# One edit to a hand-placed schedule: recurrent groups a slot sooner, and a new order around the first MLP products

## The chip, the cores and the metric

The kernel runs on one core of a Trainium2 chip. The metric is the device time of one execution in microseconds (us), less being better. Five instruction engines take part: TensorE (PE in the profile; its weight loads are PEld), VectorE (DVE), ScalarE (ACT), GpSimd (POOL) and SyncE (SP), which here issues the DMA transfers.

## The reference

Two parts follow one another. The first is an mLSTM cell over `(batch, heads, tokens, width) = (4, 8, 768, 40)`; per token, with stabilised gates:

```python
m_new  = np.maximum(f_gate + m, i_gate)
f_stab = np.exp(f_gate + m - m_new); i_stab = np.exp(i_gate - m_new); m = m_new
C = f_stab * C + i_stab * (v outer k)
n = f_stab * n + i_stab * k
y = sigmoid(o_gate) * (C @ q) / np.maximum(np.abs(n @ q), 1.0)
```

The second takes the result as `x` of shape `(4, 768, 320)`:

```python
mixed = np.real(fft(fft(x, axis=1), axis=2))
u  = x + mixed
un = (u - mean) / np.sqrt(var + 1e-06)
out = u + np.maximum(un @ w_ch1, 0.0) @ w_ch2      # 320 -> 1280 -> 320
```

All is float32.

## The kernel before

**The stages.** Each of the four batches (b = 0 to 3) runs through a recurrence, a Fourier mix and an MLP. The recurrence is done in six chunks (c = 0 to 5) of 128 tokens. For b = 1 to 3 it works on halves of 64 tokens: `halves_scores` and `halves_to_state` (products into the bank `ps`), `halves_from_state`, `halves_between` and `halves_from_chunk` (into the bank `ph`). All these products are issued by the helper `product`, at L582, so that the trace has them under that line. One chunk's products, together with the `from` products of an earlier chunk, make a group of small products of 40 or 64 rows and 40 or 64 columns.

What surrounds a group runs on other engines. ACT does `mlstm_exp` (L551, the weights W, eight instructions for the eight heads) and the gate in `mlstm_tanh` (L748, L650). POOL does `mlstm_scale_q` (L563, qg), `mlstm_scale_v` (L569, vw), `mlstm_mask` (L578) and the decay of the state (L705, C). DVE does `halves_add` (L712, C), `halves_weigh` (L717, W) and `mlstm_finish` (L768 to L772 and L759, which turn `ph` into `x`). SP issues the loads (qk, kvt, W, so, Gb).

**The mix** has sequence transforms (`mix_seq`, `mix_tail`, L944 and L956, banks pz and pzt; those of pzt have 64 columns), feature transforms (`mix_feat`, L990, bank pu), `mix_add` (DVE, L1003 to L1014: adds pu to x and takes the statistics), `mix_center` (ACT, L1028, uc), `mix_turn` (PE, L1039, transposes into ph or put) and `mix_turn_out` (ACT, L1044, uT).

**The MLP** of batch 0 is `mlp_in` (L1137, with `mlp_in_rests` for the last 64 features, L1120 through `rest_products`), `mlp_relu` (ACT, L1155) and `mlp_out` (L1275). Batches 1 to 3 use five blocks i = 0 to 4 with fewer products on sums of operands. `mlp_block` (L1203) has steps 0, 1, 2, 2.5 and 3: its products write four banks `pm`, ACT copies them out (L1218, L1232, L1241 and, with the relu, L1254), DVE adds (L1209), step 2.5 issues sixteen 64-feature products (L1120), and `mlp_relu_in_place` (L1258) follows. The output is `mlp_out_pair` (L1332) with three parts n of four steps, on `hidden_sums` (L1317, S1 to S4) and with `residual` (DVE, L1281).

**Weights.** They come in pieces that are stored packed: `load` (SP, L453), `take` (DVE, L463 and L465), `convert` (ACT, L471) and `join` (DVE, L478, L481 and L485). The list `when` gives the slots of take, convert and join of each piece.

**The order** is written by hand. `at(slot, phase, fn)` notes a step, and `run` issues all steps in sorted order; every engine's queue is then in that order:

```python
    def run(end=None):
        for key in sorted(plan):
            if end is None or key[0] < end:
                for fn, args in plan.pop(key):
                    fn(*args)

    EVAC, FILL, MAIN, FILL_PE = range(4)
```

Batch 0's `mlp_in` has slots 31 to 50 and its `mlp_out` 51 to 62. The blocks of batch 1 have 63 to 82 (i=0 is 63 to 66, i=1 67 to 70), its `mlp_out_pair` 83 to 94, the blocks of batch 2 95 to 114. `plan_halves` starts at slot 32 for b=1, 54 for b=2 and 86 for b=3, with three slots for a chunk. So b=1's recurrence runs beside the first batch's MLP input, b=2's beside its output and the first blocks of batch 1 (about 105 to 193 us), b=3's beside the output of batch 1 and the blocks of batch 2 (about 193 to 277 us).

Of the kernel before, what the change touches and what calls it, by code (L numbers as in the profile page):

```python
# [20 lines left out]
NT = S // L  # L21
NP = H // 2
# [35 lines left out]
def kernel(  # L58
# [68 lines left out]
    def at(slot, phase, fn, *args):  # L127
        plan.setdefault((slot, phase), []).append((fn, args))
# [7 lines left out]
    EVAC, FILL, MAIN, FILL_PE = range(4)  # L136
# [682 lines left out]
    def plan_halves(b, s0, stride=3):  # L819
        at(s0 - 2, FILL + 0.7, halves_start, b)  # L820
        for c in range(NT):
            s = s0 + stride * c
            end = c == NT - 1
            t = 22 + 2 * c if b == 1 and c < 3 else s - 6
            at(t, FILL, mlstm_load, b, c)
            at(t, FILL, mlstm_load_max, b, c)
            at(*((t, FILL + 0.02) if (b, c) == (1, 0) else (t + 1 if c < 2 or b > 1 else s - 5, FILL)), mlstm_load_decay, b, c)
            at(s - 2, FILL, mlstm_load_o, b, c)
            at(s - 2, FILL + 0.1, mlstm_scale_q, b, c)
            at(s - 2, FILL + 0.15, halves_alone, b, c)  # L830
            at(s - 1, FILL, mlstm_scale_v, b, c)
            early = (b, c) == (1, 0)
            at(*((27, FILL + 0.227) if early else (s - 1, FILL)), mlstm_exp, b, c, 0)
            at(*((32, EVAC + 0.15) if early else (s - 1, FILL + 0.5)), mlstm_exp, b, c, NP)
            at(s, FILL, mlstm_mask, b, c)
            at(s, FILL_PE + 2.05, halves_scores, b, c)
            at(s, FILL_PE + 2.5, halves_to_state, b, c)
            for i in range(2):
                at(s + i, FILL + 0.05, halves_decay, b, c, i)
                at(s + 1 + i, FILL - 0.2, halves_add, b, c, i)  # L840
            at(s + 1, FILL, halves_weigh, b, c)
            if end:
                for fn, phase in (((halves_from_state, -0.3), (halves_between, -0.2), (halves_from_chunk, -0.05)) if b == 1 else
                                  ((halves_from_state, 0.1), (halves_between, 0.15), (halves_from_chunk, 0.3))):
                    at(s + (3 if b == 1 else 4), MAIN + phase, fn, b, c)
            else:
                at(s + 3, FILL_PE, halves_from_state, b, c)
                at(s + 3, FILL_PE + 0.5, halves_between, b, c)
                at(s + 3, FILL_PE + 3, halves_from_chunk, b, c)
            at(s + 3, FILL_PE + 0.6, mlstm_tanh, b, c)  # L850
            at(s + 4, FILL + 0.05 if b == 1 else MAIN + 0.4, mlstm_finish, b, c)

# [213 lines left out]
    def plan_mix(b, s0, x_done, s_feat, s_add, s_turn):  # L1068
        for j in range(TG):
            p = TG - 1 - j  # L1070
            if b == 0:
                at((17, 18, 18.5)[j], FILL + (0.1, 0.07, 0.3)[j], mix_fold, b, p)
                s, phase = ((17, 3), (19, 3), (22, 4))[j]
                for i, part in enumerate(((1,), (0,)) if j == 1 else ((0, 1),)):
                    at(s, FILL_PE + phase + 0.1 * i, mix_seq, b, p, part)
                at(*((18, FILL_PE + 0.2) if j == 0 else (s, FILL_PE + phase + 0.2)), mix_tail, b, p)
            else:
                at(x_done[j] + (b > 1 and j == TG - 1), FILL + 0.5 if b < 2 else FILL_PE + 0.2, mix_fold, b, p)
            if b > 0 and j == 0:
                for step in range(2):  # L1080
                    at(*((x_done[-1], FILL + 0.55) if b == 1 else (x_done[-1] + 2 + 2 * step, FILL_PE + 0.25)),
                       mix_fold_again, b, step)
                at(s0, FILL_PE + 4, mix_seq, b, p, (0,))
                at(s0 + 1, FILL_PE + 4, mix_seq, b, p, (1,))
                at(s0 + 2, FILL_PE + 4, mix_tail, b, p)
        for i in range(2):
            at(s0 + 1 if b == 0 else s0 + 1 + i, FILL, mix_seq_out, b, i)
        at(s0 + (1 if b == 0 else 3), FILL + 0.1, mix_tail_out, b)
        for p in range(TG):
            for i in range(3) if b == 0 and p == TG - 1 else ():  # L1090
                at(s_feat[p] + i, FILL_PE + 5.1, mix_feat, b, p, slice(i, i + 1))
            if b == 0 and p == TG - 2:
                at(s_feat[p], FILL_PE + 4.06, mix_feat, b, p, slice(0, 3))
                at(s_feat[p] + 1, FILL_PE + 4.95, mix_feat, b, p, slice(3, 5))
            elif b == 0 and p == 0:
                at(s_feat[p], FILL_PE + 4, mix_feat, b, p, slice(0, 2))
                at(s_feat[p], FILL_PE + 4.04, mix_feat, b, p, slice(2, 3))
            elif b > 0 or p < TG - 1:
                at(s_feat[p], FILL_PE + 4, mix_feat, b, p)
        for c, a, t in zip(ORDER, s_add, s_turn):  # L1100
            at(a, FILL if b < 2 else MAIN + 0.5, mix_add, b, c)
            if b > 0 and c == TG - 2:
                at(a, FILL + 0.15 if b < 2 else MAIN + 0.55, mix_own, b)
            at(*(((32, EVAC + 0.1) if c == 3 else (a, FILL + 0.225) if c in (4, 2) else (t, FILL + 0.1)) if b == 0 else
                 (t, FILL + 0.1)), mix_center, b, c)
            at(t, FILL_PE + (5 if b == 0 or c in ORDER[:4] else -0.1), mix_turn, b, c)
            if b > 0:
                at(t, FILL_PE + 6, mix_turn_out, b, c)
            elif t < s_mlp:
                at(t + 1, FILL + 0.2, mix_turn_out, b, c)  # L1110
            else:
                at(t + 1, EVAC, mix_turn_out, b, c)
# [254 lines left out]
    def plan_mlp(b, s):  # L1367
# [10 lines left out]
        for gr, n in IN_ORDER if b == 0 else ():  # L1378
            for f in (2 * n, 2 * n + 1):
                at(s, MAIN, mlp_in, b, gr, f)  # L1380
                s += 1
            i = IN_ORDER.index((gr, n))
            if i < 4 or i % 2 == 0 or i == 9:
                at(*((s, MAIN + 0.5) if i == 1 else (s - 1, MAIN + (-0.1 if i in (2, 8, 9) else 0.2))), mlp_in_rests, b, i,
                   False)
                if 3 < i < 8:
                    at(s - 1, MAIN + 0.25, mlp_in_rests, b, i + 1, True)
            for f in (2 * n, 2 * n + 1):
                at(s + (i == 1), EVAC, mlp_relu, b, gr, f)
        if b > 0:  # L1390
            for j in range(1, 5):
                at(s - (5, 4, 3, 3)[j - 1], FILL_PE + 0.3, hidden_sums, 0, (j,), 0, NFF // 2 - 2)
# [9 lines left out]
        for gr in groups if b == 0 else ():  # L1402
            for i in range(TG):
# [3 lines left out]
                n = gr * TG + i  # L1407
# [45 lines left out]
        at(66 if n == 3 else 57, FILL + 0.41, out_weight_sums, n)  # L1453

    when = [((2, 0.7), (4, 0.5), None), ((18.5, 0.7), (20, 0.7), (21, 0.6)), ((21.5, 0.7), (23, 0.15), None)]
    when += [((27, 0.16), None, (29, 0.5)), ((30, 0.7), (34, 0.7), (35, 0.6))]
    when += [((s, 0.7), (s + 1, 0.7), (s + 2, 0.6)) for s in (36, 39, 42, 48, 51)]
    pieces = w1_pieces + w2_pieces
    for n, (w, p) in enumerate(zip(when, pieces)):
        if n > 2:  # L1460
            at(when[n - 2][2][0] + 1 if n != 4 else 27, FILL + 0.7, p.load)
        for t, fn in zip(w, (p.take, p.convert, p.join)):
            if t:
                at(t[0], FILL + t[1], fn)
    for part, s in enumerate((7, 10, 13)):
        at(s, FILL - 0.28, pieces[0].join, part)
    for part, (s, phase) in enumerate(((27, 0.13), (27, 0.14), (27, 0.15))):
        at(s, FILL + phase, pieces[2].join, part)
    at(27, FILL + 0.23, pieces[3].convert)

    early = [(3, mlstm_load, 3), (3, mlstm_load_o, 2), (4, mlstm_load, 4), (5, mlstm_load_decay, 3),
             (5, mlstm_load_decay, 4), (7, mlstm_load_o, 3), (7, mlstm_load, 5),
             (11, mlstm_load_decay, 5), (11, mlstm_load_o, 4), (12, load_tables, None), (15, None, 2),
             (11.5, mlstm_load_o, 5)]
# [157 lines left out]
```

## Time and profile before

| | |
|---|---|
| time, median of 3 runs | 383.31 us (382.96 to 384.71) |
| time of the profiled execution | 381.6 us |
| its span | 379.7 us |
| PE busy | 372.2 us, 98% of the span |
| DVE, ACT, POOL busy | 74%, 45%, 35% |
| granted TensorE clock | 1.0 throughout |
| data moved | 43.99 MB, mean 116 GB/s |

The span goes from the first to the last instruction of one profiled execution; its time also holds what lies around the span. "Busy" adds up the instructions of an engine; for PE the ends of the matrix products are modelled. A row of the timeline has the start, the duration, engine, line, operation, output and inputs, tile and shape, and in brackets the idle time ahead of it and who ended it. A float32 product shows as two instructions.

### The profile page before, as it was taken

How to read it: one execution, taken by the hardware profiler on the slowest of the kernel's cores; microseconds unless marked ns; L12 is line 12 of the kernel's file. 1: busy time of each engine (PE TensorE's matmuls, PEld its weight loads, DVE VectorE, ACT ScalarE, POOL GpSimd, SP SyncE). 2: the span in 40 equal slices, each digit the busy share in tenths (PEclk: the TensorE clock that was granted, in tenths of full speed). 3: DMA queues.
4: the chain of work that ended last, by engine and by line, in shares of the span. 5: the costliest groups of instructions: out<-in, count | busy, mean ns of one | idle time of the engine just before them, and what ended most of it. 6: DMA issues, size and time to landing. Idle time of an engine off the chain costs nothing.

```text
span 379.7 us, 11405 instructions
## 1 busy us (share of the span) xinstructions
PE 372.2 (98%) x4602; PEld 274.3 (72%) x4602; DVE 279.4 (74%) x662; ACT 170.9 (45%) x501; POOL 131.7 (35%) x238
## 2 busy tenths in 40 slices
PE   8999998999999999999999999999999999999996
PEld 5888565566677777566588999566588996546996
DVE  8798899899997596787965787878745885245552
ACT  5978766657332224654542054564520233544000
POOL 5665423965695014561602424651300000020000
PEclk9999999999999999999999999999999999999999
DMA  7979499698971244464003534440000001000011
GB/s 203 292 219 344 125 251 269 174 270 246 260 212 38 90 128 128 129 187 139 0 3 93 157 117 130 131 80 3 0 2 35 19 18 36 0 0 2 35 36 35
DMA packets 21760, 43.99 MB, mean 116 GB/s; under 512 B 3508, under 2 KB 9996, under 8 KB 21580
## 3 DMA queue, kind: packets, MB, share of 16 engines
q1 hardware_dynamic: 21708, 43.27, 39.3%
q8 instruction: 36, 0.59, 0.7%
q14 instruction: 16, 0.13, 0.1%
HBM read 39.16 MB, written 4.10 MB: 114 GB/s over the span
## 4 chain that ended last, share of the span: by engine, by line
PE 83%; DVE 5%; POOL 3%; ACT 1%; DMA 1%; issue 1%; POOLq 0%; DVEq 0%
PE po L1332 22%; PE pm L1203 19%; PE po L1275 9%; PE pm L1120 7%; PE ph L582 5%; PE pm L1137 4%; PE ps L582 4%; PE pu L990 3%; PE pz L944 2%; PE put L1039 2%; DMA raw<-in_w 1%; PE hb L582 1%; PE pzt L944 1%; POOL W L578 1%; PE pz L956 1%
## 5 line engine op out<-in xcount | busy, mean ns | idle before, releaser
L1281 DVE SCALAR_TENSOR_TENSOR x<-po,rstd,x 128x160 f32<-128x160 f32 (+1 forms) x69 | 27.1, 394 | 37.6 <-PE po L1332 34.0
L1209 DVE TENSOR_TENSOR h<-h,pm 128x384 f32<-128x384 f32 x60 | 30.5, 549 | 24.1 <-PE pm L1120 10.8
L578 POOL TENSOR_SCALAR_AFFINE_SELECT W<-W 64x512 f32<-64x512 f32 x36 | 28.5, 792 | 42.1 <-ACT W L551 23.2
L1203 PE MATMUL pm<-uT,w_sb 128*128 128x384 f32 x90 | 37.5, 506 | 0.1
L551 ACT ACTIVATE W<-W,colT 128x64 f32<-128x64 f32 x144 | 36.6, 336 | 0.1
L705 POOL TENSOR_TENSOR C<-C,decB 128x164 f32<-128x164 f32 x33 | 18.1, 550 | 49.8 <-DVE C L712 45.6
L1275 PE MATMUL po<-w_sb,h 128*128 128x320 f32 x120 | 33.9, 433 | 0.0
L1120 PE MATMUL pm<-uT,w_sb 64*64 64x384 f32 x320 | 32.7, 497 | 0.0
L563 POOL TENSOR_TENSOR qg<-qk,Gb 128x512 f32<-128x512 f32 x21 | 27.7, 1318 | 8.3 <-DMA Gb<-G_d 7.0
L1063 POOL TENSOR_TENSOR t<-rstd 128x6 f32<-128x6 f32 x12 | 3.7, 311 | 75.5 <-DVE v L1057 75.0
L1137 PE MATMUL pm<-uT,w_sb 128*128 128x384 f32 x80 | 28.9, 499 | 0.6 <-ACT h L1155 0.6
L1275 PEld LDWEIGHTS po<-w_sb,h 128*128 128x128 f32 x120 | 22.4, 190 | 9.1 <-issue 0.3
L1332 PE MATMUL po<-T,S 128*128 128x160 f32 x180 | 27.8, 301 | 0.2 <-DVE x L1281 0.2
L1332 PEld LDWEIGHTS po<-T,S 128*128 128x128 f32 x180 | 25.4, 190 | 1.3 <-DVE x L1281 0.4
L1332 PE MATMUL po<-w_sb,h 128*128 128x160 f32 x180 | 26.3, 300 | 0.0
L1332 PEld LDWEIGHTS po<-w_sb,h 128*128 128x128 f32 x180 | 25.2, 190 | 1.4 <-DVE x L1281 0.3
L1203 PEld LDWEIGHTS pm<-uT,w_sb 128*128 128x128 f32 x90 | 15.5, 189 | 12.8 <-DVE h L1209 5.3
L1258 ACT ACTIVATE h<-h 128x384 f32<-128x384 f32 x45 | 23.1, 520 | 2.9 <-DVE h L1209 2.9
L1120 PEld LDWEIGHTS pm<-uT,w_sb 64*64 64x64 f32 x320 | 10.9, 132 | 16.4 <-issue 13.6
L1137 PEld LDWEIGHTS pm<-uT,w_sb 128*128 128x128 f32 x80 | 14.1, 189 | 11.4 <-issue 1.8
L569 POOL TENSOR_TENSOR vw<-kvt,colT 128x328 f32<-128x328 f32 x23 | 19.3, 839 | 4.0 <-issue 2.2
L582 PE MATMUL ps<-qk 40*64 40x64 f32 (+1 forms) x768 | 19.1, 235 | 0.4 <-DVE C L712 0.4
(254 smaller groups left out, 814.3 us busy)
## 6 DMA issues: line engine op xcount, KB each, us to landing
kvt<-in_kv SPq DMA_DIRECT2D x24, 336.0 KB
qk<-in_qkT SPq DMA_DIRECT2D x48, 160.0 KB
raw<-in_w SPq DMA_DIRECT2D x10, 640.0 KB
Gb<-G_d SPq DMA_DIRECT2D x42, 128.0 KB
W<-M_d SPq DMA_DIRECT2D x36, 128.0 KB
so<-in_o SPq DMA_DIRECT2D x24, 160.0 KB
out<-x SPq DMA_DIRECT2D x23, 160.0 KB
ds_sb<-in_dft_s SPq DMA_DIRECT2D x1, 1158.0 KB
```

What stands on the lines that cost most here:

```text
L551: nc.scalar.activation(out=k.W[:, h, :], in_=M, func=AF.Exp, scale=-1.0, bias=colT[:, c, 0, b * H + h:b * H + h + 1])
L563: nc.gpsimd.tensor_tensor(out=k.qg[:, :, t], in0=k.qk[:, 0, :, t], in1=k.Gb[:, :, t], op=OP.mult)
L578: nc.gpsimd.affine_select(out=W, in_=W, compare_op=OP.is_ge, fill=0.0, base=base, pattern=[[0, H], [-1 if back else 1, LH]], channel_multi ...
L582: nc.tensor.matmul(out, w, x, start=start, stop=True, skip_group_check=True)
L1120: nc.tensor.matmul(banks[i][half(cols)], w1_rest(n)[half(i), half(cols)], u[half(i)], start=start, stop=not start, skip_group_check=True)
L1137: nc.tensor.matmul(k.pm[i], w1_block(ch, f // 2 * 2 + i), u[2 * ch], start=(ch == 0 and not ahead), stop=(ch == 1 and (ahead or n in (2, 8 ...
L1203: nc.tensor.matmul(bank, w, u, start=start, stop=True, skip_group_check=True)
L1209: nc.vector.tensor_tensor(out=h, in0=h, in1=bank, op=OP.add)
L1258: nc.scalar.activation(out=h, in_=h, func=AF.Relu, scale=-1.0)
L1275: nc.tensor.matmul(k.po[m], hidden(gr, f)[:, i * L:(i + 1) * L], w2_sb[:, f, :], start=(f == 0), stop=(f == NFF - 1))
L1281: nc.vector.scalar_tensor_tensor(out=u, in0=po, scalar=k.rstd[:, c:c + 1], in1=u, op0=OP.mult, op1=OP.add)
L1332: nc.tensor.matmul(po, a[:, f], w[:, f], start=start and f == 0, stop=f == half - 1, skip_group_check=True)
```

## The change

Two groups of edits.

*First batch* (recurrence b=1, beside batch 0's `mlp_in`). `mix_center` of c=3 goes from slot 32 to 33. The relus of `mlp_in`'s block i=0 go one slot and phase ahead of where they stood. The exponentials of the second four heads of (b=1, c=0) move from slot 32 to 28, `mlstm_scale_v` of (1, 1) two slots ahead. Of the weights' pieces, piece 2's join goes from 27 to 28, piece 3's take, convert and join from 27, 27 and 29 to 28, 32 and 33, piece 4's take from 30 to 33, piece 5's take from 36 to 35, and the loads of pieces 4 and 5 to 28 and 33. PE's order in this part is the same as before.

*Third and fourth batch* (recurrence b=2 and b=3). All steps of chunks c = 0 to 4 come one slot sooner, with their loads. The `from` products, the tanh and the finish of a chunk follow its new slot, except that c=4's stay where they were (`follow`). The exponentials of c=4 and c=5 come one further slot sooner (`ahead`). PE gets the groups in these places: for b=2, c=0 into `mlp_out`, c=1 beside the products of pzt, c=2 ahead of the mix's first transpose, c=3 right ahead of block i=0, c=4 right behind the 64-feature products (L1120) of block i=0 instead of behind step 3; for b=3, c=0 ahead of pzt, c=1 between step 1 and step 2 of `mlp_out_pair`, c=2 behind step 0 of n=2, c=3 ahead of the block, c=4 behind the 64-feature products.

On ACT the eight exponentials of c=4 then stand ahead of L1218 of block i=0 (they stood between L1232 and L1241), and those of c=5 between L1254 and the first L1258 of block i=1. On DVE of b=3's part, the finish of c=0 and of c=1 come ahead of a `mix_add` that they followed. On SP the stores (L1283) and the loads of a chunk swap places in several cases.

```diff
@@ plan_halves @@
         for c in range(NT):
-            s = s0 + stride * c
+            s = s0 + stride * c - (b > 1 and c < NT - 1)
             end = c == NT - 1
+            follow = s + 3 + (b > 1 and c == NT - 2)
...
-            at(s - 1, FILL, mlstm_scale_v, b, c)
-            early = (b, c) == (1, 0)
-            at(*((27, FILL + 0.227) if early else (s - 1, FILL)), mlstm_exp, b, c, 0)
-            at(*((32, EVAC + 0.15) if early else (s - 1, FILL + 0.5)), mlstm_exp, b, c, NP)
+            at(*((s - 3, FILL + 0.06) if (b, c) == (1, 1) else (s - 1, FILL)), mlstm_scale_v, b, c)
+            early, ahead = (b, c) == (1, 0), int(b > 1 and c >= NT - 2)
+            at(*((27, FILL + 0.227) if early else (s - 1 - ahead, FILL)), mlstm_exp, b, c, 0)
+            at(*((28, FILL + 0.23) if early else (s - 1 - ahead, FILL + 0.5)), mlstm_exp, b, c, NP)
...
-                at(s + 3, FILL_PE, halves_from_state, b, c)
-                at(s + 3, FILL_PE + 0.5, halves_between, b, c)
-                at(s + 3, FILL_PE + 3, halves_from_chunk, b, c)
-            at(s + 3, FILL_PE + 0.6, mlstm_tanh, b, c)
-            at(s + 4, FILL + 0.05 if b == 1 else MAIN + 0.4, mlstm_finish, b, c)
+                at(follow, FILL_PE, halves_from_state, b, c)
+                at(follow, FILL_PE + 0.5, halves_between, b, c)
+                at(follow, FILL_PE + 3, halves_from_chunk, b, c)
+            at(follow, FILL_PE + 0.6, mlstm_tanh, b, c)
+            at(follow + 1, FILL + 0.05 if b == 1 else MAIN + 0.4, mlstm_finish, b, c)
@@ plan_mix @@
-            at(*(((32, EVAC + 0.1) if c == 3 else (a, FILL + 0.225) if c in (4, 2) else (t, FILL + 0.1)) if b == 0 else
+            at(*(((33, EVAC + 0.1) if c == 3 else (a, FILL + 0.225) if c in (4, 2) else (t, FILL + 0.1)) if b == 0 else
@@ plan_mlp @@
-                at(s + (i == 1), EVAC, mlp_relu, b, gr, f)
+                at(*((s - 1, MAIN + 0.3) if i == 0 else (s + (i == 1), EVAC)), mlp_relu, b, gr, f)
@@ weight pieces @@
-    when += [((27, 0.16), None, (29, 0.5)), ((30, 0.7), (34, 0.7), (35, 0.6))]
-    when += [((s, 0.7), (s + 1, 0.7), (s + 2, 0.6)) for s in (36, 39, 42, 48, 51)]
+    when += [((28, 0.2), None, (33, -0.9)), ((33, 0.7), (34, 0.7), (35, 0.6))]
+    when += [((35, 0.65) if s == 36 else (s, 0.7), (s + 1, 0.7), (s + 2, 0.6)) for s in (36, 39, 42, 48, 51)]
...
-            at(when[n - 2][2][0] + 1 if n != 4 else 27, FILL + 0.7, p.load)
+            at({4: 28, 5: 33}[n] if n in (4, 5) else when[n - 2][2][0] + 1, FILL + 0.7, p.load)
...
-    for part, (s, phase) in enumerate(((27, 0.13), (27, 0.14), (27, 0.15))):
+    for part, (s, phase) in enumerate(((28, 0.1), (28, 0.11), (28, 0.12))):
...
-    at(27, FILL + 0.23, pieces[3].convert)
+    at(32, MAIN + 0.35, pieces[3].convert)
```

## The prediction

> **What bounds the kernel now.** I read the page's busy times first, then its chain, then the timeline around the lines that the diff touches. Each line number below is one of the kernel before; from the edit in `plan_halves` on, the changed kernel's are higher by one. b counts batches from 0, c the chunks of a recurrence.
>
> ```profile
> span 379.7 us, 11405 instructions
> PE 372.2 (98%) x4602; PEld 274.3 (72%) x4602; DVE 279.4 (74%) x662; ACT 170.9 (45%) x501; POOL 131.7 (35%) x238
> PE 83%; DVE 5%; POOL 3%; ACT 1%; DMA 1%; issue 1%; POOLq 0%; DVEq 0%
> ```
>
> PE is the bound: 98% of the span, 83% of the chain that ended last. No matrix product is added or removed, so time can only come from PE's waits and from what products cost beside one another. The waits that the timeline states are few, and three lie where the first edits are:
>
> ```profile
> 59.82 0.61 ACT L1028 ACTIVATE uc<-x 128x384 f32<-128x384 f32 x1 [0.78 <-DVE x L1014]
> 60.85 0.55 PE L1039 MATMUL ph<-ident,uc 128*128 128x128 f32 x3 [0.57 <-ACT uT L1044]
> 63.31 0.91 PE L1137 MATMUL pm<-uT,w_sb 128*128 128x384 f32 x2 [0.62 <-ACT h L1155]
> 76.19 0.69 PE L582 MATMUL ps<-qk 40*64 40x64 f32 x32 [0.37 <-DVE C L712]
> ```
>
> The columns are start, duration, engine, line, operation, and in brackets the idle time with its releaser. Other waits are hidden inside a group of products whose first operand was there and whose later one was not. Sixteen 64-feature products (L1120) show it, in block i=0 and in i=1:
>
> ```profile
> 160.10 2.31 PE L1120 MATMUL pm<-uT,w_sb 64*64 64x384 f32 x16
> 169.13 1.55 PE L1120 MATMUL pm<-uT,w_sb 64*64 64x384 f32 x16
> 159.10 2.02 ACT L551 ACTIVATE W<-W,colT 128x64 f32<-128x64 f32 x8
> 161.03 0.46 ACT L1241 COPY h<-pm 128x384 f32<-128x384 f32 x1
> ```
>
> From start to the next start the first is 2.24 and the second 1.34: 0.9 lost, because the copy L1241, which empties the bank that the last of the sixteen write, stood behind eight exponentials (W x8, 2.02). The same group at 244.12 in the next batch loses as much.
>
> **First batch** (recurrence of b=1 beside the first MLP stage). PE's order stays; DVE's and ACT's change. Now DVE does a piece's join and take from 55.27 to 58.50 and only then mix_add of c=2 (58.50 to 59.73); uc of c=2 follows at 59.82. After, that mix_add comes first, 3.2 sooner. By the rows' durations uc ends at 57.6, W x4 (1.05) at 58.65, the turn's copy and both relus (0.86) at 60.3, so the stalls of 0.57 and 0.62 at 60.85 and 63.31 go. from_state of c=0 then starts at 66.6 instead of 67.95 (1.35 sooner). The next from_state, now at 74.69, starts on finish (DVE, ended 74.63); with the piece-4 take behind C and W of c=0, finish ends near 73.8. The third stall (0.37) goes because piece 5's take (L463 and L465, 1.28) no longer precedes that C. The group after it ends at 76.1 instead of 77.60: 1.5 sooner. DVE has no idle from 71.97 to 119.2, so PE cannot keep more than DVE gains; by the same chain piece 5's L478 starts at 74.0 instead of 76.06, a gain of 2.06, which is the upper end. POOL's mask and vw move across the conversions: L478, L481 and L485 take 1.18, 1.31, 1.11 beside POOL and 0.79, 0.81, 0.82 alone, 1.18 in all, of which half may come back (1.2 - 0.6 = 0.6 as the lower end). SP's moved loads (two weight pieces, so) cover ahead of need; a late piece would show as DVE's wait on raw, now 0.64 at 63.78, which is inside that bound. **Taken: -1.4 (from -2.0 to -0.6).**
>
> **Third batch's recurrence (b=2), 150 to 170 us.** Five groups go a slot up. A group's entry costs little: L1275 x10 takes 2.69, and 2.79 ahead of a group; the group's last part (kvt,W) is 0.58 with 128*128 work behind it and 0.46 with 64*64 behind it; pu costs 1.19 after a group and 1.08 else. Group c=1 beside pzt (64 columns) saves 0.3 at most, c=2 0.06, c=4 beside L1120 about 0.2. Each exp comes a slot sooner on ACT: W x8 (2.0) of c=4 is now ahead of L1218 of block i=0, and no longer between L1232 and L1241. That frees the sixteen rests (0.9) and 0.3 ahead of them, but the product behind L1218 waits about 0.65 and the rests' bank waits for an L1209 that now stands behind a finish (1.65), about 0.85. So i=0 gives -0.2 + 1.5 - 1.2 = +0.1. In i=1 the order is now L1218, L1254 (0.49), W x8 (2.0), L1258 (0.5), L1232 (0.46); before, W x8 (165.45 to 167.45) lay beside group c=4, which now is ahead of step 3. The product that needs L1232's bank is wanted 2.6 after step 3 and gets it after 3.5: +0.87. **Sum -0.36 + 0.1 + 0.87 = +0.6 (from -0.4 to +1.5).**
>
> [...]
>
> **Fourth batch's recurrence (b=3), 200 to 250 us.** Group c=0 beside pzt saves 0.25. Group c=1 now stands between steps 1 and 2 of mlp_out_pair, where step 2 lost 0.15 of stated gap and 0.2 inside at 216.63; that goes, -0.35, and 0.07 at joins: -0.67 by 220.75. Then DVE:
>
> ```profile
> 221.62 0.79 DVE L1317 TENSOR_TENSOR S<-h,h 128x640 f32<-128x640 f32 x1
> 224.02 0.37 DVE L1281 SCALAR_TENSOR_TENSOR x<-po,rstd,x 128x160 f32<-128x160 f32 x1
> 223.17 0.71 PE L990 MATMUL pu<-dd_sb,Z 128*128 128x161 f32 x4
> ```
>
> Before, step 2's residual ended at 220.0, mix_add (1.65) ran to 221.6, and pu at 223.17 found its bank free by 1.5. After, step 2 lies behind the group and its residual ends near 221.2; finish of c=0 (1.65, as at 236.38 to 238.02) comes ahead of mix_add, whose last read of the bank ends at 224.1, while pu is wanted at 222.4: 1.7. The next step 0 needs the residual behind S, S (1.57) and C (0.25), 0.1 late: **+1.8** in all. The same pattern, finish of c=1 ahead of mix_add of the last chunk, makes its transpose late: residual at 234.3, then 1.64 + 1.65 + uc 0.6 gives 238.2 against 237.1 wanted, **+1.0**. Block i=0 loses both its stalls (-1.2: its W x8 is early enough) and i=1 gains 0.87. **Sum -0.67 + 1.8 + 1.0 - 1.2 + 0.87 = +1.8 (from 0.2 to 2.6);** the low end has finish in DVE's idle times, where it would cost nothing. From 277 us on no order changes.
>
> **Sum.** -1.4 + 0.6 + 1.8 = +1.0; I take +0.9, since the pu wait gives slack to what is queued behind it. The profiled execution took 381.6 (span 379.7 and 1.9 around it) and so becomes 382.5; the median, 383.31, lies 1.7 above that one, so on its basis 384.2.
>
> **Rivals.** (1) *DVE and ACT run ahead and hide the new waits* (faster): if finish's five small operations fall in DVE's idle slots (0.82 at 219.65, 1.29 at 234.72), b=3 gives -0.67 - 1.2 + 0.87 = -1.0 in place of +1.8 and b=2 its -0.36 + 0.1. With -1.4 that is -2.7: 380.6. Against it: finish stands in order behind a residual that PE makes at 221, not at 219. It decides at pu's start: no gap there, and this is it. (2) *DVE and POOL collide in the first batch* (slower): the gain ahead of 72 us is eaten when vw and the mask meet the moved conversions; two masks cost 2.44 beside them and 1.38 apart, three conversions 3.6 and 2.42, together 2.24, more than the 1.4 taken. With nothing gained there the sum is +2.4: 385.7. It decides if PE reaches the group at 76.19 no sooner than now. For it: DVE has no slack from 71.97 on. (3) *No change*: PE is gapless after 77.6, and the first batch pays what the others cost: 383.3.
>
> [...]
>
> **How the numbers follow.** The forecast has a chance of 0.47, rival 1 0.18, rival 2 0.23, rival 3 0.12. A measurement of this kernel can tell 0.5% (1.9 us) from no change, so the bounds are 381.4 and 385.2. Faster: rival 1 (most of it) and a low tail of the forecast, 0.18. Slower: rival 2 and the upper quarter of the forecast, 0.35. The rest, 0.47, is within. The forecast's own range, with the three sums half way to their ends, is 382.6 to 385.8. The whole range reaches down into rival 1, to 381.3 (its better half, 0.11, is left out), and up past rival 2 (385.7) to 386.4, where the upper ends of the last two sums meet (0.08 is left out above).
>
> **What would show it.** Right: the gaps at 60.85, 63.31 and 76.19 gone and the group after them 1.4 sooner; the sixteen rests of i=0 back at 1.35 in b=3's block; a DVE-released gap of 1.7 before the third pu of b=3's mix; 0.9 inside the products of i=1 of both blocks. Wrong: no gap at that pu, or the same 1.35 us late start of from_state of c=0 as before.

## The result, and the profile after

The changed kernel takes 390.02 us (median of 4 runs, 388.37 to 391.40) against 383.21 us; the ratio is 1.0156, 95% interval 1.0125 to 1.0187. It is slower by 6.8 us; the forecast was 384.2, with 386.4 as its upper end. The profiled execution took 391.4, so it is one of the longer ones; the profile of before (381.6) is one of the shorter ones of its kernel. In the changed kernel all lines from the edit on are higher by one (L1120 is L1121, L1332 is L1333).

The page of after, its span, the busy times and the chain by engine:

```profile
span 389.1 us, 11415 instructions
PE 375.1 (96%) x4602; PEld 277.0 (71%) x4602; DVE 284.9 (73%) x662; ACT 170.7 (44%) x501; POOL 134.9 (35%) x238
PE 80%; DVE 7%; ACT 4%; issue 3%; DMA 3%; POOL 3%; SPq 0%; POOLq 0%; DVEq 0%; ACTq 0%
```

The same 9204 instructions run on PE, but it is no longer gapless: its share of the chain falls from 83% to 80%, and ACT and "issue" rise from 1% each to 4% and 3%. PE's waits in after (engine, line and what it waited for, then sum, count and longest; "issue" is idle time in which PE waited for nothing that the profile shows):

```profile
PE ph L582 <- issue: 1.9, 1, 1.9
PE pu L991 <- DVE x L1012: 1.4, 1, 1.4
PE pm L1204 <- ACT h L1233: 1.4, 2, 0.7
PE ph L582 <- POOL vw L569: 0.9, 1, 0.9
PE put L1040 <- ACT uc L1029: 0.8, 1, 0.8
PE ph L582 <- ACT warm L748: 0.7, 1, 0.7
PE po L1333 <- DVE x L1282: 0.6, 1, 0.6
PE pm L1121 <- DVE h L1210: 0.5, 1, 0.5
```

The two gaps of the first batch are gone, as forecast. These rows answer to the ones at 60.85 and 63.31 before; the third answers to the group at 74.69:

```profile
60.40 0.55 PE L1040 MATMUL ph<-ident,uc 128*128 128x128 f32 x3
60.78 2.10 PE L1138 MATMUL pm<-uT,w_sb 128*128 128x384 f32 x6
74.62 0.60 PE L582 MATMUL ph<-C,qg 40*64 40x41 f32 x26 [0.94 <-POOL vw L569]
```

PE was 1.24 us early at 63 us, but waited 0.94 at 74.62 and started that group only 0.07 sooner than before. Comparing the starts of the same products in both traces gives the whole account (after minus before; a group that was moved counts where both traces have passed it):

| stretch | forecast | trace |
|---|---|---|
| first batch, at 63 us / 77.6 us / 105 us | -1.4 at the end | -1.24 / -0.64 / -0.08 |
| b=2, joins up to block i=0 | -0.36 | -0.2 |
| b=2, block i=0 | +0.1 | +0.65 |
| b=2, block i=1 | +0.87 | +0.73 |
| b=3, c=0 and c=1, up to 221 us | -0.67 | +0.4 |
| b=3, third pu and the po behind it | +1.8 | +2.36 |
| b=3, last transpose | +1.0 | +1.0, and 0.2 at one before |
| b=3, block i=0 | -1.2 | +3.2 |
| b=3, block i=1 | +0.87 | +0.73 |

The rows differ from the forecast by 8.0 us in all. Two thirds of that are two rows: block i=0 of b=3, where 1.2 was to be won and 3.2 was lost, and the stretch to 221 us; the first batch's lost gain is another 1.3. Block i=0 is in this timeline of after, with the table of windows below (window, its length, busy time and count of PE, PEld, DVE, ACT and POOL, then granted clock, DMA share and GB/s):

```profile
252.56 0.51 PE L582 MATMUL ph<-kvt,W 64*64 64x41 f32 x20
254.96 0.65 PE L582 MATMUL ph<-kvt,W 64*64 64x41 f32 x11 [1.89 <-issue]
```

```profile
250.00:252.00 2.00, 2.00 (x65) 1.51 (x67) 1.12 (x3) 0.13 (x1) 1.17 (x3) 1.00 0.93 200
252.00:254.00 2.00, 1.07 (x83) 0.95 (x73) 1.29 (x3) 0.52 (x2) 0.46 (x1) 1.00 1.01 249
254.00:256.00 2.00, 1.04 (x12) 0.96 (x12) 0.24 (x2) 0.00 (x0) 0.00 (x0) 0.71 0.26 62
256.00:258.00 2.00, 2.00 (x4) 1.05 (x4) 1.83 (x4) 0.48 (x1) 1.81 (x2) 0.50 0.04 8
```

PE stops for 1.89 us inside 32 like products for which the profile shows no wait for an operand, while the DMA share is 1.01 (252 to 254 us); then its clock is 0.71 and 0.50 in the two windows up to 258 us. The author's reading, which early_loads below bears out, is that it lacked instructions. The page lists a queue of kind "instruction" (packets, MB, share of the DMA engines):

```profile
q8 instruction: 36, 0.59, 0.7%
```

In the trace each of the 36 packets has 16 KB. That they are PE's is not stated there; taken as PE's alone they give 64 bytes to each of its 9204 instructions and 256 instructions to a packet, an estimate from these numbers. One such packet starts at 243.37 and the next at 252.22; in between PE starts 449 instructions, where no two packets elsewhere in either trace are more than 365 apart. In the kernel before, packets start at 245.87 and at 250.54.

### The profile page after: what moved, and what is told of

Its sections match the earlier page's. It is cut to its first block, busy times and chain, and to the rows that moved or that the text cites. A ratio compares the mean times of both kernels' runs of the same rounds, so it can differ in the third digit from the quotient of the medians.

```text
span 389.1 us, 11415 instructions
## 1 busy us (share of the span) xinstructions
PE 375.1 (96%) x4602; PEld 277.0 (71%) x4602; DVE 284.9 (73%) x662; ACT 170.7 (44%) x501; POOL 134.9 (35%) x238
## 4 chain that ended last, share of the span: by engine, by line
PE 80%; DVE 7%; ACT 4%; issue 3%; DMA 3%; POOL 3%; SPq 0%; POOLq 0%; DVEq 0%; ACTq 0%
PE po L1333 21%; PE pm L1204 17%; PE po L1276 8%; PE pm L1121 7%; PE ph L582 5%; PE pm L1138 4%; PE ps L582 4%; PE pu L991 3%; PE pz L945 2%; DMA so<-in_o 2%; PE put L1040 1%; ACT W L551 1%; PE hb L582 1%; PE pzt L945 1%; PE pi L142 1%
## 5 line engine op out<-in xcount | busy, mean ns | idle before, releaser
L1210 DVE TENSOR_TENSOR h<-h,pm 128x384 f32<-128x384 f32 x60 | 30.5, 550 | 28.4 <-PE pm L1121 13.4
L578 POOL TENSOR_SCALAR_AFFINE_SELECT W<-W 64x512 f32<-64x512 f32 x36 | 29.3, 815 | 39.7 <-ACT W L551 37.7
L1121 PE MATMUL pm<-uT,w_sb 64*64 64x384 f32 x320 | 32.8, 496 | 0.5 <-DVE h L1210 0.5
L1333 PE MATMUL po<-T,S 128*128 128x160 f32 x180 | 27.8, 301 | 0.0
L1333 PE MATMUL po<-w_sb,h 128*128 128x160 f32 x180 | 26.6, 301 | 0.6 <-DVE x L1282 0.6
L1333 PEld LDWEIGHTS po<-w_sb,h 128*128 128x128 f32 x180 | 25.2, 190 | 2.3 <-DVE x L1282 1.1
L1333 PEld LDWEIGHTS po<-T,S 128*128 128x128 f32 x180 | 25.4, 190 | 0.9
L1204 PEld LDWEIGHTS pm<-uT,w_sb 128*128 128x128 f32 x90 | 16.2, 194 | 13.0 <-DVE h L1210 4.1
L1121 PEld LDWEIGHTS pm<-uT,w_sb 64*64 64x64 f32 x320 | 11.3, 132 | 16.5 <-issue 13.6
L1138 PEld LDWEIGHTS pm<-uT,w_sb 128*128 128x128 f32 x80 | 14.2, 190 | 10.5 <-issue 1.8
L569 POOL TENSOR_TENSOR vw<-kvt,colT 128x328 f32<-128x328 f32 x23 | 20.2, 878 | 4.2 <-issue 2.2
L1318 DVE TENSOR_TENSOR S<-h,h 128x640 f32<-128x640 f32 (+2 forms) x24 | 16.8, 700 | 4.0 <-ACT h L1259 4.0
```

The source lines that it names most:

```text
L578: nc.gpsimd.affine_select(out=W, in_=W, compare_op=OP.is_ge, fill=0.0, base=base, pattern=[[0, H], [-1 if back else 1, LH]], channel_multi ...
L1121: nc.tensor.matmul(banks[i][half(cols)], w1_rest(n)[half(i), half(cols)], u[half(i)], start=start, stop=not start, skip_group_check=True)
L1138: nc.tensor.matmul(k.pm[i], w1_block(ch, f // 2 * 2 + i), u[2 * ch], start=(ch == 0 and not ahead), stop=(ch == 1 and (ahead or n in (2, 8 ...
L1204: nc.tensor.matmul(bank, w, u, start=start, stop=True, skip_group_check=True)
L1210: nc.vector.tensor_tensor(out=h, in0=h, in1=bank, op=OP.add)
L1333: nc.tensor.matmul(po, a[:, f], w[:, f], start=start and f == 0, stop=f == half - 1, skip_group_check=True)
```

## The experiments

**The change in its parts.** Four kernels on one chip: the whole change once more, and each part alone. The edits replace the condition of the shifted groups:

```diff
-            s = s0 + stride * c - (b > 1 and c < NT - 1)
-            follow = s + 3 + (b > 1 and c == NT - 2)
-            ... int(b > 1 and c >= NT - 2)
+            s = s0 + stride * c - (b == 2 and c < NT - 1)        # third_only; b == 3 in fourth_only
+            follow = s + 3 + (b == 2 and c == NT - 2)
+            ... int(b == 2 and c >= NT - 2)
```

first_only has these terms off and the other edits in; third_only and fourth_only have the first batch as before the change.

> The whole change once more. Theory 1 (PE is starved of instructions when 449 instructions lie between two of its 16 KB fetches, behind the L1121 rests of the fourth part's block i=0, and the clock then halves): the trace shows again an 'issue' gap of 0.5 to 2 us inside the kvt,W products of group c=4 of b=3 near 253 us, and a time of 388 to 391. Theory 2 (that gap was one execution's accident, and the steady loss is the waits alone): no such gap, span near 386, time near 388.

Measured: 390.93 us (388.64 to 393.65, 6 runs) against 384.08; ratio 1.0192 (1.0147 to 1.0237). The gap is there again, in the same group, and this time with the clock at 1.0:

```profile
256.40 0.43 PE L582 MATMUL ph<-kvt,W 64*64 64x41 f32 x11 [1.53 <-issue]
```

So it is no accident of one execution. In both traces PE stops behind the same instruction, the 7361st of its queue.

> The edits of the first batch alone. Theory 1 (VectorE has no slack from 72 us on and gives PE back only what it gained itself): the two gaps near 61 and 63 us go, PE is 1.2 us early at 63 and 0.1 to 0.3 early at 105; time 0.0 to 0.4 below the kernel before. Rival (as predicted, 1.4 kept): 1.2 to 1.5 below.

Measured: 383.12 us; ratio 0.9976 (0.9945 to 1.0008), not told from no change. In its trace the gaps are gone, and at 105 us nothing of the gain is left (PE is 0.27 late). The trace goes with theory 1, but the medians lie 0.96 apart, more than it explains; this is taken up with before_again.

> The edits of b=2 alone (first batch and b=3 as before). Theory 1 (waits add up): +1.3, of it 0.7 in block i=1 behind L1232 and about 0.5 to 0.9 in block i=0 where the rests wait for L1209 behind the finish. Rival (its loads also disturb the part after it, or the part only costs together with the first batch's edits): +0.3 or less, or above +2.

Measured: 385.27 us, +1.2; ratio 1.0043 (1.0016 to 1.0070). The trace has 0.68 behind L1233 in i=1 and 0.49 behind L1210 in i=0: theory 1.

> The edits of b=3 alone. Theory 1 (instruction starvation and waits): +5 to +8: waits of about 0.7 (kvt,W behind L748), 1.4 (pu), 0.6 (po), 0.8 (put), 0.7 (block i=1), and the gap with the slow clock, 3, in some executions. Theory 2 (waits alone): +4.2 to +5, clock 1.0. The prediction's own sum was +1.8.

Measured: 388.43 us, +4.35; ratio 1.0135 (1.0093 to 1.0177). All five waits are there with the same sizes, the issue gap is only 0.3, and no clock loss in the profile: by these numbers the waits alone are 4 to 5 (theory 2). The three parts add up to -0.96 + 1.19 + 4.35 = 4.6; the whole change on the same chip costs 6.85. The missing 2.3 are of the size of what the pause costs in the traces of the whole change (3.2 in the first, of it 1.9 gap and 1.3 slow products behind it); with six runs of each that is an argument, not a measurement.

**One wait at a time.** Four kernels, each the whole change with one more edit. They ran on another chip than full_again, so the differences to it are differences of medians between chips, and the traces count for more.

```diff
 early_loads
-            t = 22 + 2 * c if b == 1 and c < 3 else s - 6
+            t = 22 + 2 * c if b == 1 and c < 3 else s - 6 - ((b, c) == (3, NT - 1))
 finish_later
-            at(follow + 1, FILL + 0.05 if b == 1 else MAIN + 0.4, mlstm_finish, b, c)
+            at(follow + 1 + (b == 3 and c < 2), FILL + 0.05 if b == 1 else MAIN + 0.4, mlstm_finish, b, c)
 own_later
-                at(a, FILL + 0.15 if b < 2 else MAIN + 0.55, mix_own, b)
+                at(a, FILL + 0.15 if b < 2 else FILL_PE + 0.7 if b == 2 else MAIN + 0.55, mix_own, b)
 exp_earlier
-            ... int(b > 1 and c >= NT - 2)
+            ... (b > 1) * max(0, c - NT + 3)
```

> The whole change, but the loads of b=3's chunk c=5 (qk, kvt, W, Gb) stand ahead of the store that follows step 3 of the output stage, not behind it; that store made SyncE wait until 246 us and pushed 0.8 MB of loads into the 247 to 254 us in which TensorE's 16 KB fetch of instructions falls. Theory 1 (the fetch is queued behind those loads): the issue gap in group c=4 (1.9 and 1.5 in the two profiles of the whole change) falls below 0.4 and the time falls by 1.5 to 3 against the whole change (390 to 391), to 388 to 389.5; the clock stays 1.0. Rival (the starvation comes from the density of small products alone, 400 to 450 instructions in 9 us): the gap stays between 1.3 and 2.

Of the four loads Gb stayed behind the store, so three moved. Measured: 388.18 us (12 runs), ratio 1.0127 (1.0093 to 1.0160) against 1.0192 for the whole change: 2.75 less by the medians, though the intervals overlap a little. PE runs through the group without a gap, and the DMA share at 250 to 252 us is 0.51 instead of 0.93:

```profile
252.47 0.67 PE L582 MATMUL ph<-kvt,W 64*64 64x41 f32 x31
253.06 0.91 PE L1204 MATMUL pm<-uT,w_sb 128*128 128x384 f32 x2
```

```profile
250.00:252.00 2.00, 2.00 (x72) 1.51 (x75) 1.21 (x3) 0.07 (x2) 1.12 (x2) 1.00 0.51 159
```

The instruction packet now starts at 250.28, 231 instructions behind the one before. PE's order and the density of its products are unchanged, so the loads decide, not the density alone. It is shown that the packet starts sooner and the pause is gone when the loads are elsewhere; how the DMA engines choose between them isn't visible in the trace.

The place of the group has its part too. The packet starts soonest when PE is at its 7110th instruction (all_mended; 7115 in early_loads). From there to the 7361st PE needs 2.5 us in early_loads, and as much in after and full_again up to the pause; in the kernel before, where c=4's group comes later, it needs 4.2. Against the 7110th instruction the packet starts 0.0 us late in early_loads, 0.7 in before, 1.56 in full_again and 1.87 in after. In the last two PE goes on 2.7 us after the packet's start. So before had room for a late packet, with its DMA engines just as full:

```profile
248.00:250.00 2.00, 2.00 (x129) 1.95 (x126) 0.54 (x2) 1.76 (x6) 0.13 (x1) 1.00 1.00 188
```

The number of instructions between two packets does not tell a stall by itself: before_again has 451 of them between the packets at 70.19 and 78.48 us and no pause there, own_later stops for 1.53 us with 376.

> The whole change, but the finish of c=0 and of c=1 of b=3 a slot later, behind mix_add, as before the change. Theory (finish ahead of mix_add is what the prediction said): the waits at the third pu (1.44), at po (0.57) and at the last put (0.84) go, 2.4 to 2.9 less than the whole change, so about 388. Rival (the bank is late for another reason, the residual that PE makes later): the pu wait stays above 0.7.

Measured: 386.52 us, ratio 1.0069 (1.0037 to 1.0100): 4.4 less than the whole change. The waits at pu, po and put are gone from PE's list, which is 2.85; the packet also came almost in time (at 248.05, with 0.14 of idle time left at the same instruction), as PE reached that group sooner. The theory holds, the rival falls: the third pu waited for mix_add behind the finish. One small wait takes their place, for the finish itself:

```profile
PE ph L582 <- DVE x L759: 0.4, 1, 0.4
```

> The whole change, but mix_own of b=2 (two ScalarE copies, L1020 and L1021) behind the tanh of b=3's c=0. Theory: the wait of 0.74 of the kvt,W products at 219.6 us was for L748, which stood behind mix_own, which waited for mix_add; it goes, and by 221 us the part has gained 0.2 over its place before the change instead of losing 0.5. Time 0.7 less than the whole change. Rival (the wait is for the mask or another operand): it stays at 0.5 or more.

Measured: 388.97 us, ratio 1.0109 (1.0053 to 1.0165). In after, the copy L748 stood behind mix_own's L1020, which waited for mix_add; here it goes first:

```profile
219.43 0.14 ACT L748 COPY warm<-ph 1x1 f32<-1x1 f32 x1
```

```profile
218.32 0.15 ACT L748 COPY warm<-ph 1x1 f32<-1x1 f32 x1 [8.00 <-PE ph L582]
219.02 0.24 ACT L1020 COPY pu<-pu 1x161 f32<-1x161 f32 x1 [0.18 <-DVE x L1012]
```

The first line is after, the other two own_later. The wait of 0.74 is gone, and over the stretch to 221 us PE gains 0.5 on the kernel before instead of losing 0.4. The time fell by more than the 0.7 expected, but this profile has the gap again (1.5, clock 0.995), so the total, with its six runs, says little; the trace decides.

> The whole change, but the eight exponentials of c=5 (b=2 and b=3) one more slot ahead, in front of L1219 and L1255 instead of between L1255 and L1259. Theory: the 0.68 that the S3 product of block i=1 waits for L1233 goes in both blocks: 1.4 less than the whole change. Rival (the exponentials then delay L1219, whose bank the next products want): a new wait of 0.3 or more at step 1 of block i=1, and less than 0.7 gained.

Measured: 389.18 us, ratio 1.0114 (1.0063 to 1.0166). Here the rival is half right: both waits of 0.68 for L1233 are gone, and a new one stands in their place.

```profile
PE pm L1204 <- ACT h L1219: 0.4, 1, 0.4
```

In b=3's block the step is +0.50 instead of +0.73. The total moved by 1.7, of which the trace gives 0.2 to this edit in that block; the gap was 0.7 in its profile.

**The mends together.** all_mended has them all, with two changes: the exponentials of c=5 go right behind the last copy of block i=0 (slot s-4, MAIN+0.3), and the finish of c=2 goes behind the first L1210 of that block. first_fourth is the same without b=2's edits. first_take is the first batch's edits alone with one of them undone:

```diff
-    when += [((35, 0.65) if s == 36 else (s, 0.7), (s + 1, 0.7), (s + 2, 0.6)) for s in (36, 39, 42, 48, 51)]
+    when += [((s, 0.7), (s + 1, 0.7), (s + 2, 0.6)) for s in (36, 39, 42, 48, 51)]
```

> The whole change with every wait named so far taken away by order alone: loads of b=3's c=5 ahead of the store, finish of b=3's c=0 and c=1 behind mix_add, mix_own behind the tanh, finish of c=2 (b=2, b=3) behind the first L1210 of block i=0, exponentials of c=5 right behind the last copy of block i=0. Theory (the loss is these five waits and the starved fetch, about 1.9 + 2.9 + 0.7 + 0.5 + 1.4 us, and nothing else): 7 less than the whole change, within 1 us of the kernel before or up to 1 below, 383 to 385. Rival (the new order is worse in itself, and other waits take their place): 386 or more.

Measured: 383.46 us, ratio 0.9986 (0.9954 to 1.0017). Within 0.5 of the kernel before: the named waits and the pause are the loss. One wait grew (ph for L748, 1.1 in its list); eight exponentials now stand ahead of a tanh, which may be why.

> The first batch's edits and b=3's edits with the same mends; b=2's recurrence as before the change. Theory: the first batch's edits are worth about -0.9 by the medians, b=3's mended part about -0.5 (block i=0 no longer waits for its copy): 382.5 to 383.5, the fastest of all. Rival: b=3's new places are no better than the old ones, and it ties with the first batch's edits alone, 383 to 384.

Measured: 381.64 us (380.82 to 385.55, 12 runs), ratio 0.9942 (0.9914 to 0.9969): 0.6% faster than the kernel before, and below what either theory gave.

> The first batch's edits alone, but piece 5's take (L463 and L465, 0.98) again behind the finish, where it was before the change. Theory (VectorE's queue sets the from_state at 74.6 to 74.9 us, and a step put ahead of finish there costs PE what it lasts): from_state starts 0.6 to 1.0 sooner, of which the C behind the take costs 0.4 again; 0.3 to 0.6 better than the first batch's edits alone by 77.6 us. Rival (GpSimd's vw is what PE waits for, and it does not move): from_state no sooner, and PE later by 0.4 at 77.6.

Measured: 383.17 us, ratio 0.9976 (0.9951 to 1.0001); first_only had 0.9976. The group that waited 0.94 now starts a microsecond sooner (73.54 against 74.62 in after and 74.69 before):

```profile
73.54 0.68 PE L582 MATMUL ph<-C,qg 40*64 40x41 f32 x32
```

PE is 1.24 early at 77.6 us, more than was expected, and 0.17 early at 85.8. So DVE's order did set this start, and the gain is given back a little later all the same: 0.70 of it in the sixteen 64-feature products at 79 to 81 us, which take 2.15 from start to next start here and 1.45 in before, and 0.37 in the group behind them. The first loss goes with the start of an instruction packet. The packet that starts ahead of these products starts 1.94 us ahead of them here, 2.14 in after, where they take 1.87, and 3.04 in before. Of the sixteen profiles, the six in which it starts at most 2.14 ahead have 1.87 to 2.58 for them, and the five in which it starts 2.72 or more ahead have 1.45 each. In third_only part of it is put down to "issue" (0.28). No run moves this packet alone, so the cause is argued here, not shown.

**What is left.** Three more runs. mended_fourth is first_fourth without the first batch's edits, best is first_fourth with first_take's line, before_again is the kernel before.

> The first batch's edits with piece 5's take left behind the finish, and b=3's edits with the five mends; b=2 as before the change. Theory (VectorE gives back by 105 us whatever the first part gains): no better than with the take ahead, 381 to 382.5, first and fourth part together 0.4 to 0.8% below the kernel before. Rival (the earlier from_state, 1.2 us early at 77.6 instead of 0.6, is kept): 381.0 or less.

Measured: 381.46 us (379.98 to 385.21, 12 runs), ratio 0.9945 (0.9912 to 0.9978), the same as first_fourth within the intervals: the theory.

> b=3's edits with the five mends alone. Theory A (the gain of the combined kernel comes from b=3: its loads no longer meet TensorE's fetch of instructions, so slow executions with a lower clock become rare): 1.0 to 2.0 below the kernel before, and fewer executions with a clock under 0.997. Theory B (it comes from the first batch's edits, about -0.9, and the rest is scatter): within 0.5 of the kernel before.

Measured: 383.55 us, ratio 0.9986 (0.9959 to 1.0014). Theory B by its time: b=3's mended part alone brings at most a few tenths. Executions with a clock under 0.997 were 2 of 12, against 3 of 23 of the kernel before, so they did not become rare.

> The kernel before once more, for a second profile of it. If its first profile (381.6) was a lucky execution, this one shows 383 to 385 and its trace the wait that makes the difference (an issue gap inside a group of recurrent products, or a weight piece that lands late near 61 to 74 us); if not, the span is again 379.5 to 380.5.

Measured: 383.96 us, span 381.9, 2.2 more than the first profile. Half of the difference is in one place, at DVE's wait for a piece of the weights:

```profile
65.42 0.49 DVE L463 TENSOR_SCALAR e<-raw 128x640 uint32<-128x640 uint32 x1 [1.83 <-DMA raw<-in_w]
```

and in PE's list of waits:

```profile
PE ps L582 <- POOL vw L569: 0.9, 1, 0.9
```

In the first profile that wait was 0.64 and PE lost nothing here. The C and W of chunk c=0 stood behind this take, POOL's decay, qg and vw behind that C, PE behind vw: 1.09 us by 69.65. fourth_only, with the old order there, has it too (1.90 on raw, 1.14 lost). The new order puts the first C and W ahead of the take; DVE's wait on raw was 0.97 in first_only, and PE lost 0.2 there. It is no full cure: in first_fourth the piece came as late (1.81 on raw), and PE waited 1.27 for the second C, which stands behind the take. Of the five profiles with the old order two lost over 1 us here, of the eleven with the new order one; that is too few to call the new order safer.

## Why the prediction was wrong

- *The waits that came from an order (right in place, near in size).* The third pu: 1.7 forecast, 1.55 in the offsets and 1.44 as the stated gap. The last transpose: +1.0 and +1.03. Block i=1: +0.87 and +0.73, twice. All three were read from the order of DVE or ACT and durations of rows, and finish_later and exp_earlier showed the cause.
- *Mis-sized: the residual behind S, S and C.* The step had "0.1 late"; it was 0.57 stated and 0.81 in the offsets. The two sums took 1.02 and 1.16 in after, where the working had 1.57 for both; POOL's mask (226.55 to 228.39) ran beside them.
- *The step that failed first: block i=0 of b=3, -1.2.* The cover was counted, not its price. The stall of the sixteen 64-feature products (the rests) did go: in early_loads the block ends 0.5 ahead. But c=4's group behind the rests puts 449 instructions into 8.9 us, when c=5's loads fill the DMA engines (share 0.86 to 1.01 from 248 to 254 us), and the working had no term for instructions that come late. The block lost 3.2 in the profile, and the pause cost about 2.3 to 2.75 by the medians. The 251 instructions ahead of the stop took 4.2 us in before and take 2.5 after the change, so the move used up the room that a late packet had. SP's loads were looked at for the data they bring, not for what they hold up.
- *The second: "-0.67 by 220.75".* The stall in step 2 did go, but the group between steps 1 and 2 has products that wait for L748, queued on ACT behind mix_own, which waits for mix_add: 0.74. The working asked who else stands in the queue on DVE there, and not on ACT.
- *The joins (right in kind, a third too large).* A group beside pzt was to save 0.3 and 0.25. From the products ahead of pzt to those behind the pu, PE gains 0.20 in b=2 and 0.19 in b=3: the group takes 1.88 and 1.07 in either place, and what goes is 0.10 ahead of its old place and 0.11 in the pu behind it.
- *The first batch, -1.4.* The chain was right to 63 us (-1.24). finish ended at 74.47, not 73.8: C of the second half waited behind piece 4's take, whose L465 took 1.57 beside POOL's qg where the row had 0.74, and the conversions took 3.5, near the 3.6 of before. "PE cannot keep more than DVE gains" was stated as a bound and then not used for what follows 77 us; rival 2 named that end. Against the first profile -0.08 is left at 105 us; 0.42 of the 0.56 lost behind 77 us goes in the sixteen 64-feature products treated at first_take. By the medians the edits are worth 0.96 alone, which is not told from no change, and 2.1 between mended_fourth and best. The late weight piece may be part of that; no run shows how much.
- *The range.* Its upper end, 386.4, lay 0.7 above the forecast's waits with the first batch's gain lost (385.7). The narrower range of the forecast alone also has a slip: with the three sums half way to their ends it reaches up to 385.5, not 385.8. The whole range held no case in which a resource that the profile lists (DMA, instruction queue) but that never made PE wait begins to.

What stays open: whether the late packet alone takes the first part's gain between 77 and 105 us (DVE is busy for 26.30 of these 28.00 us in after, which would fit too, but no run takes work off it), and how much of the combined kernel's 2.2 to 2.5 us comes from the weight piece and how much from the instruction packets.

## What to carry to other kernels

Before a group of small instructions is moved, look how fast the engine would run through one packet of instructions there (251 in 2.5 us here, where they had 4.2) and at what the DMA engines do at that time; loads that are early enough for their data may still be in the way of the program (here the pause of 1.89 and 1.53 us was gone once three of them stood elsewhere). When a step is moved ahead on one engine, list the queue on every engine that one of its products waits for, the one-element copies too. One profile is one execution: where a wait ends on a DMA with less than a microsecond of slack, a second profile of the old kernel tells what the change is really measured against (DVE's wait on raw was 0.64 us in one and 1.83 in the other).

## What the runs showed of the hardware

- after has 36 DMA packets of kind "instruction", of 16 KB each: 256 of PE's 9204 instructions a packet, if they are PE's alone (an estimate). PE stopped with no wait for an operand shown for 1.89 and 1.53 us in two profiles of the same kernel, for 1.53, 0.7 and 0.3 in own_later, exp_earlier and fourth_only, and not at all when three loads of one chunk (qk, kvt, W) stood elsewhere. In these five PE went on 2.5 to 2.9 us after the packet had started.
- A pause of 1.89 us was followed by a clock of 0.71 and then 0.50 in the next two windows of 2 us, and four product instructions followed one another at 0.64 to 0.80 us instead of 0.32 to 0.43; after the pause of 1.53 in full_again the clock stayed at 1.00, after the one of 1.53 in own_later it was 0.51 and 0.64 in the windows from 254 to 258 us (0.995 over the whole execution). So a lower clock followed the pause in two executions and not in a third; what decides it is not shown.
